# Block-diagonal products cut into 64-row halves side by side, in a two-layer attention kernel with a hand-written order

## The chip, the cores and the metric

The kernel runs on one core of one Trainium2 chip. The metric is the time of the whole program on the device in microseconds, as the median of several runs. A profiled execution of the same program gives the times of the single instructions.

## The reference

The input `x` has 2048 tokens of width 512, in bfloat16, with 32 heads of 16. Two layers, A and B, are applied twice each: `x += A(layernorm(x))`, `x += B(layernorm(x))`, and both again with the same weights.

Layer A cuts the tokens into four segments of 512. Inside a segment it is causal softmax attention; across segments it keeps a memory `M` (16 x 16 per head) and a vector `z`:

```python
for s in range(4):
    p = softmax(qs @ ks.T * scale + mask);  a_dot = p @ vs
    pq = phi(qs)                       # phi(t) = t+1 if t > 0 else exp(t)
    a_mem = (pq @ M) / (pq @ z + 1e-6)
    o = g * a_mem + (1 - g) * a_dot    # g = sigmoid(beta), one per head
    pk = phi(ks);  M += pk.T @ vs;  z += pk.sum(0)
```

The outputs go through `wo`. In the first segment the memory is zero, so it is computed only for segments 1 to 3.

Layer B is linear attention without a mask. Queries and keys pass through a 16 x 16 matrix per head, and their features are `[softmax(p), softmax(-p)]`, 32 per head. `kv` (32 x 16 per head) and `z` are sums over all 2048 keys; `num = phi_q @ kv`, `den = phi_q @ z + 1e-6`, and `num / den` goes through `wo`.

## The kernel before

The program is a list of operations (`Graph.op`) that the Python code makes in a natural order. Each names the tiles it reads and writes. `Graph.place` then decodes a table, `ORDER`: the position of each operation in one global order, the engine of each (some copies out of PSUM may go to ScalarE or VectorE), and the buffer that each tile gets. `Graph.emit` writes one program per engine in that order, with semaphore waits where an operand comes from elsewhere. So the order on each engine is fixed by the table; nothing is chosen on the chip.

128 tokens are one step. Heads lie in groups of eight (`NG` = 4 groups, 8 x 16 = 128 partitions). Segments are indexed `s`, the steps in a segment `i`, the rounds `L` (0 and 1). In layer B the chunks of 512 tokens are `c`.

PSUM has two pools. `pD` holds two tiles of 1024 float32 (two banks each): attention scores, layer B's query projections and layer B's numerators. `pG` holds four single banks: projections, score-value products (`pv`, two of the four at a time), and a class `nz`.

Layer A's attention, `a_att`, works per step and head group. Scores of a key block (`Sd` for the diagonal, `S` for the others) are products of 64 rows: two halves of the array, each with four heads, write different banks of a D tile. ScalarE takes the exponential, and score-value products, also of 64 rows, add up in the two `pv` banks. The line of all these products is that of the helper `mm` (L325), so the profile tells them apart by tiles: `D<-pK,pQ` scores, `D<-tri,two` the causal mask, `G<-pV` and `G<-pW` score-value products.

The memory part of `a_att` (segments 1 to 3, 24 steps over both rounds) has, per step, a group `NMd` of denominator products into columns 288 to 320 of the first `pv` bank (one product of `eps32` and `onesb` for the 1e-6, and four of 8 columns, 128 rows high), a reciprocal of 32 values on VectorE (L369), a group `NM` of four products of 128 rows by 128 columns into an `nz` bank, the product with the reciprocals (L794) into a tile `nmt`, and the sum with the attention result (L796). `MSb` is the memory in block-diagonal form: each group of 128 rows holds eight heads, and a head's rows are zero outside its own 17 columns.

Layer B's `b_query` works per chunk. The queries are projected (`D<-pX,WB_q`), exponentials with both signs go into `EQ`, and `Zq` products with `Rz1` give the sums for the denominators; a short chain of ScalarE and VectorE operations on 128 columns makes two weights per head and token, `AB`. Then for each of the four steps `N` is eight products of 128 rows by 128 columns (four groups, two signs) of `EQ` with the block-diagonal `Rkv`, into a D tile (`D<-Rkv,p`). ScalarE copies it to SBUF (`Nev`), VectorE weights it (`nmul`, L961) and adds the two signs (`nadd`, L967). For the steps in `PE_T` the addition is made by TensorE, while transposing (`pair`, L808). `out_proj` transposes and multiplies with `WB["o"]`, whose rows were loaded in the order that the head layout needs.

The projections, the output products and the transposes by TensorE are 128 rows high.

The DMA queue of the SP engine carries loads, transposes (`L344`), half swaps (`pW<-pV`) and stores.

## Time and profile before

| | |
|---|---|
| median of the runs | 500.85 us (499.58, 500.85, 501.59) |
| profiled execution, first to last instruction | 497.1 us |
| around that span, by the median | 3.75 us |
| TensorE clock granted | 1.000 |
| busy: TensorE / VectorE / ScalarE / GpSimd | 469.4 / 438.1 / 440.9 / 58.8 us |
| numerators of layer B, `D<-Rkv,p` 128x128 | 256 products |
| memory products, `G<-MSb,p` 128x128 and 128x8 | 96 and 96 products |
| score and other exponentials of 1024 columns | 256, mean 1045 ns |
| loads of `WB["o"]` on SP | 4, 128 KB each |

The profile names engines PE (TensorE products), PEld (their weight loads), DVE (VectorE), ACT (ScalarE), POOL (GpSimd) and SP. A product's busy time contains the latency of the array; starts that follow each other closely tell what one costs. "64*128 64x128" is a product of 64 rows, 128 stationary columns and 128 moving columns. `p` stands for several SBUF pools, whose digits are left out.

### The profile page before, as it was taken

Reading aid. Unit: us, or ns where it says so; the run is one execution under the profiler, and the core shown is the slowest. Engines: PE = TensorE matmul, PEld = TensorE weight load, DVE = VectorE, ACT = ScalarE, POOL = GpSimd, SP = SyncE. Lnnn points to the kernel's source line nnn. Section 1 sums busy time; section 2 is a strip of 40 time slices with the busy share of each in tenths; the row PEclk is TensorE's granted clock in tenths of the full one; section 3 lists DMA queues with packets and bytes.
Section 4 is the critical chain, followed back from the end, with each engine's and each line's share of the span. In section 5 each row is a group of like instructions: output and inputs, shape, how many; then the busy total and the mean of one; then the engine's idle time right before and its main releaser. Section 6 shows DMA issues by size and latency. Waiting matters only on the chain.

```text
span 497.1 us, 22749 instructions
## 1 busy us (share of the span) xinstructions
PE 469.4 (94%) x10186; PEld 299.8 (60%) x10282; DVE 438.1 (88%) x1115; ACT 440.9 (89%) x611; POOL 58.8 (12%) x142
## 2 busy tenths in 40 slices
PE   9989999999999989999999999999999999999896
PEld 4446665566676676557555665467566757656652
DVE  7989999998778969987999999999797899889885
ACT  3889999997999989489999999999999998966992
POOL 4512201000001101001220221010001011010000
PEclk9999999999999999999999999999999999999999
DMA  8986733211112031000243444321303112110155
GB/s 227 251 142 89 81 76 47 61 27 38 41 31 53 7 47 36 12 1 1 45 75 74 82 79 69 63 47 34 58 11 50 37 34 34 26 24 2 44 113 164
DMA packets 89377, 30.20 MB, mean 61 GB/s; under 512 B 75936, under 2 KB 89280, under 8 KB 89280
## 3 DMA queue, kind: packets, MB, share of 16 engines
q1 hardware_dynamic: 88928, 28.46, 30.2%
q8 instruction: 80, 1.31, 1.1%
q10 hardware_dynamic: 288, 0.26, 0.2%
q14 instruction: 17, 0.14, 0.1%
q0 software_dynamic: 64, 0.02, 0.1%
HBM read 6.32 MB, written 2.10 MB: 17 GB/s over the span
## 4 chain that ended last, share of the span: by engine, by line
PE 61%; ACT 24%; DVE 9%; issue 3%; DMA 2%; SPq 0%; POOL 0%
PE G L325 41%; PE D L325 18%; ACT p L331 16%; ACT pE L331 6%; DMA X<-in_A_x_dram 1%; DVE p L961 1%; DVE X L826 1%; DVE pS L887 1%; DMA pX<-p 1%; DVE stats L552 1%; PE G L808 1%; DVE WA_v L508 1%; DVE pQ L642 1%; DVE pT L869 0%; ACT WB_v L339 0%
## 5 line engine op out<-in xcount | busy, mean ns | idle before, releaser
L331 ACT ACTIVATE p<-D 128x1024 bf16<-128x1024 f32 x256 | 255.6, 1045 | 13.6 <-PE D L325 12.4
L325 PE MATMUL D<-pK,pQ 64*128 64x128 bf16 (+1 forms) x2560 | 112.3, 212 | 2.9 <-ACT pE L331 0.7
L331 ACT ACTIVATE pE<-D 128x768 bf16<-128x768 f32 x128 | 104.0, 840 | 9.8 <-PE D L325 9.0
L325 PEld LDWEIGHTS D<-pK,pQ 64*128 64x128 bf16 x2560 | 70.9, 94 | 54.9 <-ACT p L331 20.5
L325 PE MATMUL G<-pV,p 64*128 64x34 bf16 (+1 forms) x1632 | 78.9, 178 | 0.5 <-ACT pE L331 0.2
L331 ACT ACTIVATE p<-G 128x512 bf16<-128x512 f32 x112 | 69.0, 633 | 7.8 <-PE G L325 7.0
L325 PEld LDWEIGHTS G<-pV,p 64*128 64x128 bf16 (+1 forms) x1632 | 70.4, 93 | 7.3 <-issue 2.6
L325 PE MATMUL G<-pV,pE 64*128 64x34 bf16 x1024 | 73.0, 175 | 1.5 <-issue 1.5
L325 PE MATMUL G<-pW,pE 64*128 64x34 bf16 x1024 | 71.3, 175 | 0.6 <-issue 0.5
L325 PE MATMUL G<-pW,p 64*128 64x34 bf16 x1536 | 70.4, 176 | 0.8 <-issue 0.8
L325 PEld LDWEIGHTS G<-pW,p 64*128 64x128 bf16 x1536 | 63.8, 93 | 0.8 <-issue 0.4
L560 POOL TENSOR_SCALAR rstd<-mv 128x1 f32<-128x1 f32 x60 | 15.5, 261 | 379.6 <-DVE mv L553 379.6
L325 PEld LDWEIGHTS G<-pV,pE 64*128 64x128 bf16 x1024 | 53.3, 93 | 3.3 <-issue 3.2
L325 PEld LDWEIGHTS G<-pW,pE 64*128 64x128 bf16 x1024 | 50.5, 92 | 0.7 <-issue 0.7
L552 DVE BATCH_NORM_STATS2 stats<-X 128x6 f32<-128x512 bf16 x64 | 43.3, 682 | 3.1 <-DMA X<-in_A_x_dram 2.5
L642 DVE TENSOR_SCALAR pQ<-p,m 128x512 bf16<-128x512 bf16 x128 | 40.8, 340 | 2.6 <-PE D L325 1.6
L887 DVE TENSOR_REDUCE pS<-p 128x32 f32<-128x512 bf16 x64 | 41.7, 671 | 0.9 <-ACT p L331 0.6
L826 DVE TENSOR_TENSOR X<-X,G 128x512 bf16<-128x512 bf16 x48 | 32.5, 682 | 10.6 <-PE G L325 10.2
L869 DVE TENSOR_TENSOR pT<-G,pT 128x1024 bf16<-128x1024 f32 x30 | 36.2, 1212 | 2.3 <-PE G L325 1.9
L562 POOL TENSOR_TENSOR rstd<-rstd,mhalf 128x1 f32<-128x1 f32 x60 | 36.0, 605 | 3.7
L325 PE MATMUL D<-tri,two 64*128 64x256 bf16 x256 | 35.1, 270 | 0.0
L325 PE MATMUL G<-WA_v,pX 128*128 128x512 bf16 x128 | 32.9, 381 | 0.6 <-DVE WA_v L508 0.5
(118 smaller groups left out, 839.6 us busy)
## 6 DMA issues: line engine op xcount, KB each, us to landing
pW<-pV SPq DMA_DIRECT2D x16, 136.0 KB, 3.2
out_dram<-X SPq DMA_DIRECT2D x16, 128.0 KB, 1.8
X<-in_A_x_dram SPq DMA_DIRECT2D x3, 512.0 KB, 7.4
pX<-in_B_wqkv_dram SPq DMA_DIRECT2D x3, 512.0 KB, 7.3
p<-p SPq DMA_TRANSPOSE x76, 2.5
pX<-p SPq DMA_TRANSPOSE x54, 2.5
WA_k<-in_A_wk_dram SPq DMA_DIRECT2D x2, 256.0 KB, 7.5
WA_v<-in_A_wv_dram SPq DMA_DIRECT2D x1, 512.0 KB, 8.4
```

What stands on the lines that cost most here:

```text
L325: ins = e.matmul(out_ap, lhsT, rhs, start=st, stop=sp, tile_position=(basep(lhsT), basep(out_ap)))
L331: return self.g.op({"act": (dur, lambda e: e.activation(out_ap(), in_ap(), func, scale=scale))}, reads, writes, opens, label=label)
L508: fn = lambda e, dt=dt: e.tensor_tensor(self.WA["v"][:, dt, :].rearrange("p (h d) -> p h d", h=H), self.WA["v"][:, dt, :].rearrange("p (h ...
L552: v(lambda e: e.bn_stats(self.stats[:, t, :], self.X[:, t, :]), 602, [R("X", t)], [R("st", t)], label="bn")
L560: v(lambda e: e.tensor_scalar(rs, self.mv[:, t, 1:2], LN_EPS, None, op0=ALU.add), 170, [R("mv", t)], [R("rstd", t)], eng="pool", label="rstd")
L562: v(lambda e: e.tensor_tensor(rs, rs, self.mhalf[:], ALU.pow), 540, [R("rstd", t), R("mhalf")], [R("rstd", t)], eng="pool", label="rstd")
L642: fn = lambda e, KM=KM, KT=KT, sl=sl: e.tensor_scalar(KM.t[:, :, sl % 2, :, 64 * (sl // 2):64 * (sl // 2) + 64], KT.t[:].rearrange("p (j h ...
L808: ins = e.matmul(tp.t[:, k * 128:(k + 1) * 128], pair.t[:, sgn * 512 + k * 128:sgn * 512 + (k + 1) * 128], self.ident[:], start=sgn == 0, ...
L826: self.v(lambda e: e.tensor_tensor(self.X[:, t, :], self.X[:, t, :], ps.t[:, 0:512], ALU.add), 602, [R("X", t), ps[0]], [R("X", t)], label ...
L869: v(lambda e: e.tensor_tensor(dst(), ps.t[:, None, 0:512].to_broadcast([128, 2, 512]).rearrange("p s (g d h) -> p s g d h", g=NG, h=8), rz ...
L887: fn = lambda e, sgn=sgn, E=E, Z=Z: e.tensor_reduce(Z.t[:, sgn * 32:(sgn + 1) * 32], E.t[:, sgn * 512:(sgn + 1) * 512].rearrange("p (h d) ...
L961: v(lambda e, Ns=Ns, Tm=Tm, w=w, shape=shape: e.tensor_tensor(shape(Tm.t[:]), shape(Ns.t[:]), w(), ALU.mult), 600, [Ns, AB[0], AB[1]], [Tm ...
```

## The change

Layer B: each numerator block becomes sixteen products of 64 rows by 64 columns, the upper and the lower half of the rows in turn, each half into its own bank of the D tile. A half holds four of a group's eight heads, so it reads only their columns of `Rkv`. Results lie by half, sign and group; the weights `AB`, the sum of the signs, the paired transposition and the rows of `WB["o"]` (loaded in eight pieces) follow that layout.

Layer A: a new function `a_mem` runs for every second step. For a segment it makes all denominators at once, 16 products of 8 columns in an `nz` bank, and takes their reciprocals on ScalarE as the exponential of a negative logarithm, kept in `Rm` (in pool `pS`). For each two steps it makes 16 products of 64 rows by 64 columns into a D tile and multiplies the 1024 results with the reciprocals on VectorE in one instruction, into a tile of pool `p2`. `a_att` only adds.

The order table is new. Decoded, it has 3017 operations where the old one has 3067: TensorE 984 (1014), ScalarE 614 (612), VectorE 1088 (1115), GpSimd 139 (138), SP 192 (188).

```diff
-        self.eps32 = sb("eps32", [128, H], BF16)
+        self.eps6 = sb("eps6", [128, 1], F32)
...
         for g in range(NG):
-            load(lambda g=g: [(self.WB["o"][:, g, :], inp["B_wo"][g * 128:(g + 1) * 128, :].rearrange("(h d) o -> d h o", d=16))],
-                 128, [R("WBo", g)])
+            for hf in range(2):
+                load(lambda g=g, hf=hf: [(self.WB["o"][64 * (g % 2):64 * (g % 2) + 64, 2 * hf + g // 2, :],
+                                          inp["B_wo"][g * 128 + hf * 64:g * 128 + hf * 64 + 64, :].rearrange("(h d) o -> d h o", d=16))],
+                     64, [R("WBo", g, hf)])
...
+    def a_mem(self, L, s, i):
...
+        if i == 0:
+            st["mem"] = []
+            Rm = st["rm"] = self.T(self.pS, "Rm")
+            mc = self.T(self.pG, "nz")
+            col = lambda q, g: mc.t[:, (q // 2) * 64:(q // 2) * 64 + 64].rearrange("p (a t g h) -> p a t g h", a=2, t=2, g=NG)[:, :, q % 2, g, :]
+            self.mm(lambda: [(col(q, g), PQ[g].t[:, q * 128:(q + 1) * 128], self.MSb[mb][:, g, :, 16], True, True)
+                             for q in range(4) for g in range(NG)], [8] * 16, list(PQ) + ms, [mc], opens=[Rm], label="NMd")
+            self.g.op({"act": (158.0, lambda e: e.activation(Rm.t[:, 0:128], mc.t[:, 0:128], ACT.Ln, bias=self.eps6[:, 0:1]))},
+                      [mc, R("eps6")], [Rm], label="mln")
+            self.act(lambda: Rm.t[:, 128:256], lambda: Rm.t[:, 0:128], ACT.Exp, 128, [Rm], [Rm], scale=-1.0, psum=False, label="mln")
+        Rm = st["rm"]
+        NM = self.T(self.pD, "S")
+        tmp = self.T(self.p2, "nmt")
+        st["mem"].append(tmp)
+        self.mm(lambda: [(NM.t[:, hf * 512 + (q - i) * 256 + g * 64:hf * 512 + (q - i) * 256 + g * 64 + 64], PQ[g].t[64 * hf:64 * hf + 64, q * 128:(q + 1) * 128],
+                          self.MSb[mb][64 * hf:64 * hf + 64, g, 4 * hf:4 * hf + 4, 0:16], True, True) for q in (i, i + 1) for g in range(NG) for hf in range(2)],
+                [], list(PQ) + ms, [NM], opens=[tmp], label="NM", rows=64, dur=240)
+        v(lambda e: e.tensor_tensor(tmp.t[:].rearrange("p (h d) -> p h d", d=16), NM.t[:, :].rearrange("p (h d) -> p h d", d=16),
+                                    Rm.t[:, 128 + 32 * i:192 + 32 * i][:, :, None].to_broadcast([128, 64, DH]), ALU.mult), 1131, [NM, Rm], [tmp], label="nmn")
...
+        if s >= 1 and i % 2 == 0:
+            self.a_mem(L, s, i)
         PV = [self.T(self.pG, "pv") for _ in range(2)]
...
-        if s >= 1:
-            PQ = st["PhQ"]
-            mc = lambda: PV[0].t[:, 288:320]
-            self.mm(lambda: [(mc(), self.onesb[:], self.eps32[:], True, False)] +
-                    [(PV[0].t[:, 288 + 8 * g:296 + 8 * g], PQ[g].t[:, i * 128:(i + 1) * 128], self.MSb[mb][:, g, :, 16], False, g == NG - 1) for g in range(NG)],
-                    [32] + [8] * 4, list(PQ) + [R("MSb", mb, 0), R("MSb", mb, 1), R("onesb"), R("eps8")], [PV[0]["d"]], label="NMd")
...
         if s >= 1:
-            v(lambda e: self.recip(e, rmem(), mc()), self.dur_recip(32), [PV[0]["d"]], [Rt[2]], label="rden")
-            NM = self.T(self.pG, "nz")
-            tmp = self.T(self.p1, "nmt")
-            self.mm(lambda: [(NM.t[:, g * 128:(g + 1) * 128], st["PhQ"][g].t[:, i * 128:(i + 1) * 128], self.MSb[mb][:, g, :, 0:16], True, True)
-                             for g in range(NG)], [128] * 4, list(st["PhQ"]) + [R("MSb", mb, 0), R("MSb", mb, 1)], [NM], opens=[tmp], label="NM")
-            v(lambda e: e.tensor_tensor(tmp.t[:].rearrange("p (h d) -> p h d", h=H), NM.t[:, :].rearrange("p (h d) -> p h d", h=H),
-                                        rmem()[:, :, None].to_broadcast([128, H, DH]), ALU.mult), 602, [NM, Rt[2]], [tmp], label="nmn")
-            v(lambda e: e.tensor_tensor(o.t[:], o.t[:], tmp.t[:], ALU.add), 335, [o[0], o[1], tmp], [o[0], o[1]], label="oadd", port=True)
+            tmp = st["mem"][i // 2]
+            hv = lambda x: x.rearrange("p (g a c) -> p a g c", g=NG, a=2)
+            mv = lambda: tmp.t[:].rearrange("p (a t g c) -> p a t g c", a=2, t=2, g=NG)[:, :, i % 2]
+            v(lambda e: e.tensor_tensor(hv(o.t[:]), hv(o.t[:]), mv(), ALU.add), 335, [o[0], o[1], tmp], [o[0], o[1]], label="oadd", port=True)
...
-            self.mm(lambda tt=tt, N=N: [(N.t[:, sgn * 512 + g * 128:sgn * 512 + (g + 1) * 128],
-                                         EQ[(g // 2, sgn)].t[:, (g % 2) * 512 + tt * 128:(g % 2) * 512 + (tt + 1) * 128],
-                                         self.Rkv[:, g * 2 + sgn, :, :], True, True) for sgn in range(2) for g in range(NG)],
-                    [128] * 8, list(EQ.values()) + [R("Rkv", q) for q in range(3)], [N], opens=[Tm] + ([] if pair else [o]), label="N")
-            shape = lambda x: x.rearrange("p (k d h) -> p k d h", k=2 * NG, h=8)
+            self.mm(lambda tt=tt, N=N: [(N.t[:, hf * 512 + sgn * 256 + g * 64:hf * 512 + sgn * 256 + (g + 1) * 64],
+                                         EQ[(g // 2, sgn)].t[64 * hf:64 * hf + 64, (g % 2) * 512 + tt * 128:(g % 2) * 512 + (tt + 1) * 128],
+                                         self.Rkv[64 * hf:64 * hf + 64, g * 2 + sgn, :, 4 * hf:4 * hf + 4], True, True)
+                                        for sgn in range(2) for g in range(NG) for hf in range(2)],
+                    [], list(EQ.values()) + [R("Rkv", q) for q in range(3)], [N], opens=[Tm] + ([] if pair else [o]), label="N", rows=64, dur=240)
+            shape = lambda x: x.rearrange("p (k d h) -> p k d h", k=4 * NG, h=4)
...
             if not pair:
-              v(lambda e, Tm=Tm, o=o: e.tensor_tensor(o.t[:], Tm.t[:, 0:512], Tm.t[:, 512:1024], ALU.add), 335, [Tm], [o], label="nadd", port=True)
+              v(lambda e, Tm=Tm, o=o: e.tensor_tensor(o.t[:].rearrange("p (a c) -> p a c", a=2), half(Tm, 0), half(Tm, 1), ALU.add), 335, [Tm], [o], label="nadd", port=True)
...
 ORDER = """
...
```

## The prediction, made before the result was known

> **What bounds the kernel now.** I read the page's busy times and its chain first, then the busy times by stage, the chain inside each stage, the matmul starts around the two product blocks that change, the groups of VectorE, and ScalarE's waits.

> The page, sections 1 and 4:

> ```profile
> PE 469.4 (94%) x10186; PEld 299.8 (60%) x10282; DVE 438.1 (88%) x1115; ACT 440.9 (89%) x611; POOL 58.8 (12%) x142
> PE 61%; ACT 24%; DVE 9%; issue 3%; DMA 2%; SPq 0%; POOL 0%
> ```

> Three engines are nearly full, and the chain runs through TensorE for 61% of the span. Busy times in five stretches (time; PE, PEld, DVE, ACT, POOL busy): layer A with memory in the first round, layer B's queries in the first round, layer A with memory in the second, the end.

> ```profile
> 75.00:205.00 130.00, 123.64 (x3261) 83.09 (x3286) 113.50 (x274) 118.99 (x157) 9.56 (x24) 1.00 0.21 38
> 205.00:275.00 70.00, 68.55 (x738) 40.41 (x748) 63.38 (x172) 62.81 (x97) 10.33 (x23) 1.00 0.18 36
> ...
> 312.00:440.00 128.00, 122.50 (x3323) 82.09 (x3349) 112.80 (x276) 118.10 (x153) 10.17 (x26) 1.00 0.22 38
> 440.00:497.00 57.00, 50.97 (x498) 30.55 (x502) 46.09 (x102) 41.75 (x62) 0.79 (x2) 1.00 0.31 75
> ```

> The chain of waits in the first two of these, by line:

> ```profile
> by line: PE G L325 57.6%; PE D L325 22.1%; ACT p L331 11.3%; ACT pE L331 4.9%; issue 4.1%; ACT pK L339 0.4%
> by line: PE G L325 53.7%; PE D L325 31.5%; ACT p L331 5.8%; PE G L808 2.7%; PE G L358 1.6%; issue 1.5%; DVE p L784 1.0%; DVE X L340 0.9%; ACT pS L331 0.7%; DVE pS L369 0.3%; DVE p L601 0.3%; DVE mv L553 0.2%
> ```

> So TensorE carries 80% of the chain in the first memory stage and 89% in the first query stage; the same view of 312 to 440 us gives it 64% (44.6 + 19.2). These shares are my weights: a microsecond taken from TensorE there is worth 0.80, 0.89 and 0.64 us. In the end stage layer B's numerators run between 460 and 485 us, and there ScalarE's timeline goes from one instruction into the next (463.5 to 476.8 us without a gap of note), so TensorE time is worth little.

> Busy TensorE time contains pipeline latency, so I price matmuls by the distance of their starts. The TensorE timeline (start, length) around a memory product, and around a numerator block of layer B:

> ```profile
> 121.31 0.33 PE L325 MATMUL D<-pK,pQ 64*128 64x128 bf16 x8
> 121.48 0.27 PE L325 MATMUL D<-tri,two 64*128 64x256 bf16 x2
> 121.69 0.41 PE L325 MATMUL G<-MSb,p 128*128 128x128 bf16 x4
> 121.93 0.18 PE L325 MATMUL G<-eps,onesb 128*128 128x32 bf16 x1
> 121.96 0.26 PE L325 MATMUL G<-MSb,p 128*128 128x8 bf16 x4
> 122.07 0.59 PE L325 MATMUL G<-WA_v,pX 128*128 128x512 bf16 x2
> ```

> ```profile
> 225.77 0.62 PE L808 MATMUL G<-ident,p 128*128 128x128 bf16 x8
> 226.23 0.61 PE L325 MATMUL D<-Rkv,p 128*128 128x128 bf16 x8
> 226.68 0.61 PE L808 MATMUL G<-ident,p 128*128 128x128 bf16 x8
> ```

> Four prices follow. (a) A 128-row numerator product takes 0.45 / 8 = 0.056 us. (b) The eight 64-row score products at 121.31 (two pairs of 128 columns, two of 64) take 0.17 us: pairs do run side by side, and a pair of 64 columns costs (0.17 - 2 x 0.056) / 2 = 0.029 us. (c) The two 256-column mask products run side by side too and need 256 / 128 x 0.056 = 0.11 us, yet the next start is 0.21 us later: going from 64-row to 128-row work costs 0.10 us. Over the 159 changes in each direction the median excess between starts is 0.096 us into 64 rows and 0.094 us out. From numerators to other 128-row work (226.23 to 226.68) it costs nothing. (d) A memory product costs 0.24 / 4 = 0.059 us, a denominator product 0.026 us.

> **Layer B numerators.** A block of eight (0.45 us) becomes eight pairs (0.23 us): 0.22 us less. But its neighbours are 128-row projections and transposes, so an isolated block now pays two changes of height, 0.19 us, and gains 0.03. Two blocks in a row (there are two D tiles to hold them) gain 0.25 together. For 32 blocks that is 1.0 to 4.0 us; the trace before has 26 runs for the 32 blocks, and with that clustering it is 7.0 - 26 x 0.19 = 2.1 us. I take 2.1, half in each round: 1.05 x 0.89 = 0.9 in the first, 0.2 in the second, where ScalarE is the limit.

> [...] Without the changes of height the first round's term would be 3.5 x 0.89 = 3.1 us and not 0.9.

> The moving operand is now read in runs of four columns, which no row shows. Bounds: 0.029 us a pair, or no overlap, 0.056; then a block saves nothing and costs 0.19 us, 6.1 us in all. I take 0.029, since runs of 16 (price d) cost only 0.003 more than contiguous columns.

> **Layer A memory products.** 96 products at 0.059 become 96 pairs at 0.029: 2.9 us less. 24 denominator groups of 0.029 + 4 x 0.026 = 0.133 us become 96 products of 0.026: 0.7 less. Striking these blocks from the sequence of starts removes 24 of the 318 changes of height (2.3 us); the six new denominator groups put back at most 12 (1.1 us), and the products now have the height of the score products beside them. Together 4.8 us, half in each round: 2.4 x 0.80 = 1.9 and 2.4 x 0.64 = 1.5.

> **VectorE and ScalarE.**

> ```profile
> L869 DVE TENSOR_TENSOR pT<-G,pT 128x1024 bf16<-128x1024 f32 x30 | 36.2, 1212 | 2.3 <-PE G L325 1.9
> L961 DVE TENSOR_TENSOR p<-p,pS 128x1024 bf16<-128x1024 bf16 x32 | 21.8, 685 | 0.5 <-ACT p L331 0.2
> L794 DVE TENSOR_TENSOR p<-G,pS 128x512 bf16<-128x512 f32 x24 | 16.4, 685 | 3.3 <-PE G L325 2.8 <-issue 0.2
> L369 DVE RECIPROCAL pS<-G 128x32 f32<-128x32 f32 x24 | 8.2, 342 | 0.2
> ```

> Gone: 24 reciprocals (8.2 us) and 24 products from PSUM (16.4). New: 12 double products, priced by the 1024-element PSUM row, 14.5. The new table's operations per engine, against those that the code adds and drops (VectorE -36, ScalarE +12), say that ten more copies go from ScalarE to VectorE (+6.9 and -6.2 us) and one weight product from VectorE to GpSimd (-1.5). The logarithm and exponential per segment cost ScalarE 6 x (0.30 + 0.32) = 3.7. VectorE -4.7, ScalarE -2.5; with chain shares of about 6% and 17% in the memory stages, 0.7 us.

> The numerators' weighting at L961 keeps its 685 ns only if runs of four weights are as good as eight. No row has four; the far bound is the 1212 ns row, 32 x 0.53 = 17 us of VectorE. I take 685, since the row it is nearest to differs only in run length. [...]

> **The price of the D tiles.** Memory products move from a G bank to one of the two D tiles through which scores reach ScalarE:

> ```profile
> ACT p L331 <- PE D L325: 12.4, 26, 3.8
> ACT pE L331 <- PE D L325: 9.0, 18, 1.4
> ```

> ScalarE waits 21.4 us in all for D today. A memory tile holds its D for 0.23 (products) + 0.2 (latency, from the 219 ns product rows) + 1.21 (the multiply), 1.6 us. Meanwhile the scores use one tile: after an exponential of 1.05 us the next needs a score block, 0.2 + 0.2 us, before it can start. That is nothing if a copy or a key exponential from G (0.6 us) lies there, 0.4 if not, 0.8 if the multiply also queues for another microsecond on VectorE. 12 tiles: 0 to 9.6 us. I take 0.1 each, 1.2, twice today's mean wait of 21.4 / 384 = 0.06 a tile.

> **At nothing.** Strided adds at L796 and L967 keep runs of 64 and 256 elements. The denominators no longer sit in a score-value bank, which frees it 0.34 us earlier, 24 times. Layer B's output weights load in eight pieces for four: four more issues of 0.6 us on SP's queue, first needed at 227 us; if they stand ahead of a transpose in the first 30 us, up to 2.4 us. The weight product on GpSimd: up to 1 us at the start.

> **The sum**: 0.9 + 0.2 + 1.9 + 1.5 + 0.7 - 1.2 = 4.0 us. The profiled execution's 497.1 us span becomes 493.1; the median of the runs, 3.75 us above that span (launch and end), goes from 500.85 to 496.9.

> **Rivals.** *Slower, by the D tiles*: each memory tile costs 0.8 us of ScalarE and its scores; 500.85 - 5.2 + 9.6 = 505.3. It decides from 0.43 us a tile (the gain is gone) and shows as slower from 0.64. For it: 21.4 us of waits on D already, and VectorE 88% full. Against: over the kernel ScalarE has 112 exponentials and some 60 copies from G to put in between. Chance 0.20. *Hidden*: ScalarE is 92% busy in both memory stages, so freed TensorE time becomes waiting and only ScalarE's 2.5 us less, partly, remains: 499.6. Chance 0.16. *The numerators lose*: no overlap; first round 3.05 x 0.89, second 0.5: 500.85 + 3.2 - 4.1 + 1.2 = 501.2. Chance 0.08. *All three engines shed alike*, with paired numerators: TensorE 8.8 of 469 us, 1.9% of the span, 491.5. Chance 0.12. The forecast has 0.44, with its own range 493.5 to 499.5.

> This kernel's measurement tells about 0.5%, 2.5 us, from no change. Faster by more: the forecast less a tail of 0.05, the last rival, 0.02 of the hidden case, 0.53. Within: 0.23. Slower: the D tiles and 0.04 of the others, 0.24. The range of 490 to 505.5 leaves out half of the D case and the ends of the others.

> **What the changed profile would show.** Right: numerator products of 64x64 about 0.03 us a pair with 0.1 us gaps around each run; ScalarE's waits for D near 22 us; the L961 form at 685 ns. Wrong: waits for D of 27 us or more, pairs of 0.056 us, or a weighting of 1.2 us.

## The result, and the profile after

The changed kernel takes 538.95 us (median of 4 runs, 532.95 to 541.87) against 500.22 us (4 runs) before. The ratio, taken without the slowest run of 541.87 us, which is also the profiled one, is 1.0717, 95% interval 1.0643 to 1.0792. It is 7% slower; 496.9 us was forecast, and the range ended at 505.5. The profiled execution of the changed kernel took 541.87 us with a span of 540.1 us, at a mean granted TensorE clock of 0.971 (before: 497.1 us, 1.000).

The page after, sections 1, 3 and 4:

```profile
PE 471.1 (87%) x10515; PEld 294.6 (55%) x10610; DVE 438.3 (81%) x1088; ACT 442.3 (82%) x613; POOL 62.9 (12%) x143
...
q8 instruction: 83, 1.36, 1.1%
...
PE 53%; DVE 20%; DMA 13%; issue 4%; ACT 4%; SPq 3%; POOL 2%; POOLq 0%; DVEq 0%
```

Busy time is what it was (TensorE 469.4, VectorE 438.1, ScalarE 440.9 us before). The 43 us are added idle time on each of the three engines. The chain shows where: DMA had 2% of it and now has 13%, GpSimd and SP's queue come in, and ScalarE falls from 24% to 4%.

The waits after (engine, line, waited for: us in total, times, longest):

```profile
ACT p L331 <- PE D L325: 29.2, 35, 4.1
...
ACT pE L331 <- PE D L325: 23.0, 31, 3.5
...
PE G L325 <- DMA pX<-p: 15.3, 10, 3.8
...
PE G L325 <- DMA p<-p: 13.5, 9, 2.8
```

ScalarE's waits for D rise from 21.4 to 52.2 us, far over the 27 us that the prediction named as the sign of its D rival. But TensorE itself now waits for transposes: with a third group (one wait of 3.8 us for `pX<-pX`) and 1.2 us of small ones 33.8 us. Before it was this one wait:

```profile
PE G L325 <- DMA pX<-p: 0.9, 1, 0.9
```

In the timeline of TensorE's two rows and SP's queue this looks so:

```profile
428.40 2.10 SPq L344 DMA_TRANSPOSE p<-p  x1
...
430.54 1.62 SPq L344 DMA_TRANSPOSE pX<-p  x1
...
434.11 1.19 SPq L344 DMA_TRANSPOSE p<-p  x1
...
435.16 0.13 PEld L325 LDWEIGHTS G<-WB_k,pX 128*128 128x128 bf16 x2 [3.96 <-DMA pX<-p]
435.16 1.46 PE L325 MATMUL G<-WB_k,pX 128*128 128x512 bf16 x3 [3.84 <-DMA pX<-p]
```

A key projection of layer B stands next in TensorE's queue. Its input was ready for transposing at 420.9 us; SP issued the transpose only at 430.5, behind others, and TensorE stood from 431.3 to 435.2.

One more row changed: the clock that TensorE was granted. In the profile before it is 1.00 throughout. After, it is 0.50 in seven stretches, 31 us in all, and six of them overlap a gap of 1.6 to 4.1 us between the starts of two weight loads or follow it within 1 us. Two stretches, the one around the end of the wait above and the next (the clock is the third number from the end):

```profile
433.66:440.49 6.83, 5.33 (x38) 2.13 (x38) 1.19 (x4) 2.49 (x4) 0.00 (x0) 0.50 0.11 20
440.49:447.00 6.51, 6.19 (x153) 3.80 (x154) 4.53 (x6) 6.19 (x9) 0.00 (x0) 1.00 0.01 3
```

In the stretches at 0.50, products of 128 rows and 512 columns start 0.43 us apart (median of 19), elsewhere 0.22 (of 781). What this is worth can only be estimated. Call a run's time multiplied by one minus its granted clock its clock loss. Over 133 runs of the kernels of this document, each compared with the others of its kernel and chip, a run with 1 us more of clock loss is 0.8 us longer. The changed kernel's four runs lose 13.1 us on average, the kernel before 0.9 to 2.2 us in its five sets of runs. By this estimate some 9 of the 38.7 us came with the clock. No run here held the clock fixed, and that the waits bring it down is not shown: at four other such gaps of the same profile, of 1.9 to 3.2 us (they end at 83.2, 277.9, 344.6 and 462.5 us), the clock is 1.00.

The prices of the new operations by form:

```profile
L985 DVE TENSOR_TENSOR p<-p,pS 128x1024 bf16<-128x1024 bf16 x32 | 21.5, 682 | 0.6 <-ACT p L331 0.5
...
L729 DVE TENSOR_TENSOR p<-D,pS 128x1024 bf16<-128x1024 f32 x12 | 14.7, 1222 | 4.6 <-PE D L325 4.1 <-ACT pS L331 0.5
...
L325 PE MATMUL D<-Rkv,p 64*128 64x64 bf16 x512 | 13.0, 201 | 0.5 <-DVE Rkv L864 0.4
```

### The profile page after: what moved, and what is told of

Same layout as the page of the kernel before. It is cut to its first block, busy times and chain, and to the rows that moved or that the text cites. A ratio compares the mean times of both kernels' runs of the same rounds, so it can differ in the third digit from the quotient of the medians.

```text
span 540.1 us, 23380 instructions
## 1 busy us (share of the span) xinstructions
PE 471.1 (87%) x10515; PEld 294.6 (55%) x10610; DVE 438.3 (81%) x1088; ACT 442.3 (82%) x613; POOL 62.9 (12%) x143
## 4 chain that ended last, share of the span: by engine, by line
PE 53%; DVE 20%; DMA 13%; issue 4%; ACT 4%; SPq 3%; POOL 2%; POOLq 0%; DVEq 0%
PE G L325 36%; PE D L325 16%; DMA pX<-p 7%; DMA p<-p 4%; ACT p L331 3%; DVE stats L554 2%; SPq L344 2%; DVE X L845 2%; DVE p L985 2%; DVE pQ L644 1%; DVE pS L906 1%; DVE pT L888 1%; DMA beta_sb<-in_A_beta_dram 1%; DMA pX<-pX 1%; DVE p L340 1%
## 5 line engine op out<-in xcount | busy, mean ns | idle before, releaser
L331 ACT ACTIVATE p<-D 128x1024 bf16<-128x1024 f32 x256 | 254.1, 1035 | 30.1 <-PE D L325 29.2
L331 ACT ACTIVATE pE<-D 128x768 bf16<-128x768 f32 x128 | 102.2, 821 | 23.4 <-PE D L325 23.0
L325 PE MATMUL D<-pK,pQ 64*128 64x128 bf16 (+1 forms) x2560 | 114.5, 214 | 2.6 <-DVE pQ L644 1.1
L325 PEld LDWEIGHTS D<-pK,pQ 64*128 64x128 bf16 x2560 | 72.5, 95 | 57.1 <-issue 23.3
L325 PE MATMUL G<-pV,p 64*128 64x34 bf16 (+1 forms) x1632 | 79.9, 179 | 3.3 <-issue 2.9
L331 ACT ACTIVATE p<-G 128x512 bf16<-128x512 f32 x112 | 67.2, 615 | 16.9 <-PE G L325 15.2
L325 PEld LDWEIGHTS G<-pV,p 64*128 64x128 bf16 (+1 forms) x1632 | 71.8, 93 | 8.8 <-issue 5.3
L325 PE MATMUL G<-pV,pE 64*128 64x34 bf16 x1024 | 73.9, 176 | 2.5 <-DMA pW<-pV 1.2
L325 PE MATMUL G<-pW,p 64*128 64x34 bf16 x1536 | 71.2, 176 | 3.0 <-issue 2.9
L325 PE MATMUL G<-pW,pE 64*128 64x34 bf16 x1024 | 72.1, 176 | 0.0
L325 PEld LDWEIGHTS G<-pW,p 64*128 64x128 bf16 x1536 | 65.1, 93 | 3.3 <-issue 2.9
L562 POOL TENSOR_SCALAR rstd<-mv 128x1 f32<-128x1 f32 x60 | 18.8, 316 | 412.8 <-DVE mv L555 405.6
L325 PEld LDWEIGHTS G<-pV,pE 64*128 64x128 bf16 x1024 | 53.9, 93 | 4.3 <-issue 2.8
L325 PEld LDWEIGHTS G<-pW,pE 64*128 64x128 bf16 x1024 | 51.1, 93 | 0.2
L325 PE MATMUL G<-WB_k,pX 128*128 128x512 bf16 x111 | 30.9, 397 | 13.4 <-DMA pX<-p 11.5
L888 DVE TENSOR_TENSOR pT<-G,pT 128x1024 bf16<-128x1024 f32 x30 | 36.2, 1215 | 5.8 <-PE G L325 5.8
L325 PE MATMUL G<-WA_o,p 128*128 128x512 bf16 x112 | 30.5, 390 | 10.6 <-DMA p<-p 7.6
L325 PE MATMUL G<-WB_o,p 128*128 128x512 bf16 x120 | 32.4, 395 | 7.0 <-DMA p<-p 5.0
```

The lines of the kernel that those rows point to most:

```text
L325: ins = e.matmul(out_ap, lhsT, rhs, start=st, stop=sp, tile_position=(basep(lhsT), basep(out_ap)))
L331: return self.g.op({"act": (dur, lambda e: e.activation(out_ap(), in_ap(), func, scale=scale))}, reads, writes, opens, label=label)
L562: v(lambda e: e.tensor_scalar(rs, self.mv[:, t, 1:2], LN_EPS, None, op0=ALU.add), 170, [R("mv", t)], [R("rstd", t)], eng="pool", label="rstd")
L888: v(lambda e: e.tensor_tensor(dst(), ps.t[:, None, 0:512].to_broadcast([128, 2, 512]).rearrange("p s (g d h) -> p s g d h", g=NG, h=8), rz ...
```

## The experiments

Two numbers are followed through all runs, besides the time. *Transposes*: the time that TensorE waits for a DMA transpose or swap (0.9 us before, 33.8 after). *Pauses*: gaps of 0.7 us and more between the starts of two weight loads, from 8 us on, where the second carries no wait on a semaphore (none before; 12 after, 12.9 us in all). The kernels of the experiments ran on four chips, each beside runs of the kernel before, whose medians there are 499.55 to 501.96 us. So kernels of different groups are better compared by their ratios than by their medians.

| kernel | us, median | ratio to before, 95% | transposes, us | pauses: number, us |
|---|---|---|---|---|
| changed | 538.95 | 1.0717 [1.0643, 1.0792] | 33.8 | 12, 12.9 |
| numerators_old_order | 503.62 | 1.0050 [1.0019, 1.0082] | 3.6 | 1, 0.7 |
| memory_old_order | 520.74 | 1.0364 [1.0266, 1.0462] | 2.6 | 5, 7.1 |
| both_old_order | 521.19 | 1.0394 [1.0328, 1.0461] | 7.4 | 6, 6.4 |
| memory_new_order | 541.65 | 1.0791 [1.0723, 1.0859] | 29.8 | 9, 10.8 |
| memory_in_G | 507.46 | 1.0143 [1.0087, 1.0199] | 0.9 | 2, 2.3 |
| wide_memory_in_D | 513.75 | 1.0271 [1.0216, 1.0325] | 1.0 | 0 |
| changed_resequenced | 523.21 | 1.0469 [1.0403, 1.0535] | 2.9 | 11, 12.8 |
| before_resequenced | 516.19 | 1.0320 [1.0262, 1.0378] | 0.6 | 2, 2.5 |
| before_shifted | 517.59 | 1.0327 [1.0258, 1.0397] | 9.1 | 9, 11.6 |
| memory_old_order_shifted | 518.70 | 1.0350 [1.0307, 1.0393] | 3.1 | 6, 6.1 |
| changed_shifted | 537.56 | 1.0723 [1.0655, 1.0791] | 27.6 | 7, 10.6 |
| changed_no_memory_products | 539.17 | 1.0756 [1.0699, 1.0813] | 32.6 | 7, 8.1 |
| before_shifted_a_packet | 500.69 | 1.0007 [0.9967, 1.0047] | 0.4 | 1, 0.7 |
| memory_in_G_aligned | 508.86 | 1.0148 [1.0087, 1.0209] | 1.3 | 1, 0.7 |
| wide_memory_in_D_aligned | 514.97 | 1.0286 [1.0218, 1.0354] | 1.9 | 0 |
| both_in_G_aligned | 509.05 | 1.0164 [1.0099, 1.0230] | 0.9 | 2, 1.7 |
| before_shifted_quarter | 508.61 | 1.0148 [1.0085, 1.0211] | 7.6 | 1, 1.3 |
| changed_shifted_quarter | 532.21 | 1.0641 [1.0573, 1.0708] | 24.9 | 9, 11.7 |

### The parts in the old order, and one part in the new

Theory: the new order table costs the time. Rival: the D tiles do, as in the prediction's slower case. Four kernels: each part alone in the old order (its new operations at the places of those that they replace), both there, and the memory part in the new order with 128-row numerators.

```diff
 both_old_order:        a_mem and N as in the change;  ORDER: old
 numerators_old_order:  N as in the change, memory as before;  ORDER: old
 memory_old_order:      a_mem as in the change, N as before;  ORDER: old
 memory_new_order:      a_mem as in the change, N as before;  ORDER: new
```

> All edits of the change, but in the old order: every operation that both kernels have keeps its place, engine and buffer of the old table; the 6 denominator groups, 12 double memory products and their multiplies are put in near the old memory products, where a D tile is free. Theory 'order' (the edits cost about nothing, the new table's sequence costs the 39 us): 496 to 508 us, TensorE waits for DMA transposes below 5 us as before. Theory 'edits' (D tiles and changes of height cost it): 520 us or more, with ScalarE waiting over 40 us for D.

> Layer B's numerators alone as 64-row pairs, with the new weight layout, all in the old order (operations one for one; the eight weight loads stand where the four stood); layer A as before. Theory 'order': 498 to 502 us, the forecast's term of about one microsecond less. Theory 'edits' by changes of height: 505 or more, about 0.2 us or more for each of 32 blocks.

> Layer A's memory part alone as in the change, in the old order with the same insertions; layer B as before. Theory 'order' with the forecast's price of a D tile: 496 to 501 us. Theory 'D tiles': each of the 12 costs 0.8 us or more, 505 us or more, and ScalarE's waits for D grow from 21 us to over 30.

> Layer B's numerators back as 128-row products, everything else as changed, in the new table's order one for one. Theory 'order': still 530 to 545 us. Theory 'numerators' (their changes of height in the new order cost it): 525 us or less.

Neither theory holds alone. The memory part costs 18 to 20 us in the old order; the new order adds 16 to 18 to the whole (1.0394 to 1.0717, 521.19 to 538.95 us). With both parts in the old order the time lies in the range of the theory "edits", but ScalarE's waits for D are 35.4 us, not over 40. The numerators alone, at 503.62 us, lie between the two ranges, some 2.5 us above before, and in the new order the kernels with and without them do not differ clearly (1.0717 and 1.0791, with intervals that overlap): they are not the cause.

How a memory product meets the D tile in memory_old_order (timeline of TensorE, VectorE, ScalarE):

```profile
345.31 0.42 PE L325 MATMUL D<-MSb,p 64*128 64x64 bf16 x16 [0.30 <-ACT pE L331]
...
345.77 1.23 DVE L727 TENSOR_TENSOR p<-D,pS 128x1024 bf16<-128x1024 f32 x1 [0.66 <-PE D L325]
...
347.05 0.45 PE L325 MATMUL D<-pK,pQ 64*128 64x128 bf16 x10 [0.36 <-DVE p L727]
...
347.49 1.02 ACT L331 ACTIVATE p<-D 128x1024 bf16<-128x1024 f32 x1 [0.16 <-PE D L325]
```

The tile is taken from 345.31 to 347.00 and the next score product starts 0.05 us later. Over the 12 tiles the hold, from the first weight load to the end of the multiply, is 1.85 us on average (the prediction's 1.6), and eleven of the 12 next score products start within 0.25 us of the release. In the changed kernel itself the next score products come 0.04 to 3.9 us after the release, and TensorE works on other products up to the start of each of the 12.

### The memory part taken apart

Theory: the D tile costs its hold. Rivals: the products of 64 rows, or the early denominators with their reciprocals on ScalarE.

```diff
 memory_in_G (old order; NMd and mln as in the change)
-        NM = self.T(self.pD, "S")          # two steps, 64 rows side by side
+        NM = self.T(self.pG, "nz")         # per step, 4 products of 128 rows
 wide_memory_in_D (table of memory_old_order)
-            NM.t[:, hf * 512 + ...], PQ[g].t[64 * hf:64 * hf + 64, ...]   # 16 of 64 x 64
+            NM.t[:, (q - i) * 512 + g * 128:...], PQ[g].t[:, ...]         # 8 of 128 x 128
```

> Layer A's memory part with the denominators of a segment in one go and their reciprocals on ACT, as in the change, but the products step by step in a bank of G at 128 rows, at the places in the order that they had before; layer B as before. D-tile theory (a memory product that takes one of the two D tiles holds up the exponentials by about 1.5 us, 12 times): no D tile is taken, so 497 to 503 us, ratio 0.99 to 1.005, and ACT's waits for PE at D return to about 21 us in all. Rival (the denominators early, the ACT reciprocals or the strided weights cost it): 512 us or more, as in memory_old_order.

> As memory_old_order, instruction for instruction in the same order and the same buffers, but the memory products of two steps are 8 products of 128 rows by 128 columns instead of 16 of 64 by 64 side by side. D-tile theory: 518 to 526 us (520.7 with 64 rows; each tile is held some 0.2 us longer and two changes of height go away). Rival (the 64-row products and their changes of height are what costs 20 us): 500 to 507 us.

Both fall between the theories, and three steps come out. **Denominators and reciprocals, 1.4%**, some 7 us, are there with no D tile taken. **The D tiles**: the two kernels have the same products, 513.75 - 507.46 = 6.3 us, 0.5 us for each of 12. **64 rows for 128**: 520.74 against 513.75 us, by the ratios 1.0364 against 1.0271, so 5 to 7 us, though the narrow version's products are shorter (0.23 us to the last start against 0.42) and its tile is held less. The two ran on different chips and their intervals overlap, so this step is the least certain of the three. The first is seen on ScalarE in memory_in_G:

```profile
165.71 1.93 ACT L331 ACTIVATE p<-D 128x1024 bf16<-128x1024 f32 x2
167.99 0.37 ACT L717 ACTIVATE pS<-G,eps 128x128 f32<-128x128 f32 x1 [0.35 <-PE G L325]
168.39 0.31 ACT L331 ACTIVATE pS<-pS 128x128 f32<-128x128 f32 x1
168.61 0.58 ACT L331 ACTIVATE p<-G 128x512 bf16<-128x512 f32 x1
```

The logarithm waits for the denominators and takes 0.37 us, the exponential 0.31, and everything behind them on ScalarE moves by that: over six segments 4.1 us of work and 1.4 of waits. The rest of the 7 us has no row of its own.

The third had no row at first: TensorE's pauses in memory_old_order are named "issue", a wait for nothing that the profile shows. There are five, 7.1 us, and none in the wide version. The clock differs too: the narrow version loses 4.0 us to it on average and the wide one 1.2, by the estimate above some 2 us of the step.

### The sequence alone

```diff
 changed_resequenced:  operations, engines and buffers of the changed kernel;  ORDER: positions sorted anew
 before_resequenced:   the same for the kernel before
```

> The changed kernel with the same instructions on the same engines in the same buffers; only the sequence of the instructions is sorted anew, by a search over single moves that replays the durations measured in the two traces. Sequence theory (the new table places products before their transposes have landed, and the memory products between two exponentials that need the D tile): the time falls below 515 us, ACT's waits for D fall from 52 us to under 30, PE's waits for transposes from 33 us to under 12. D-tile theory with a fixed price of 1.5 us a tile whatever the sequence: 518 to 525 us. If neither holds (the buffers and engines of the new table are to blame): 530 us or more.

> The kernel before, sorted anew by the same search with the same effort: what the sequence alone is worth without any edit. Sequence theory: it gains less than the changed kernel does, as its sequence was timed for its code: 485 to 500 us. If the search merely fits its own replay: 500 us or more.

The changed kernel gains 15.7 us, with no edit but the sequence. That is less than the sequence theory asked for: 523.21 us lies in the range of the D-tile theory, 518 to 525, and not below 515. Its chain and its waits:

```profile
PE 57%; DVE 23%; ACT 9%; issue 4%; DMA 3%; SPq 2%; POOL 1%; DVEq 0%
```

```profile
ACT p L331 <- PE D L325: 20.6, 41, 1.8
...
ACT pE L331 <- PE D L325: 12.4, 19, 1.5
```

The waits for transposes are gone (33.8 to 2.9 us), as the sequence theory says. ScalarE's for D fall to 33.0, not under 30; the pauses stay (12.8 us); the clock loss falls from 13.1 to 7.2 us. But the kernel before lost 16 us by the same treatment. Its second expectation holds: that search fitted its own replay of durations. With two pauses, 2.5 us, and 0.6 us of waits for transposes, no run shows what the old sequence does better. So 15.7 us is what a sequence without late transposes gives the changed kernel, not a best value. With both kernels sorted by the same search, the changed one is 7 us slower (523.21 against 516.19, on one chip).

### What the pauses are

The instruction queue moves 83 packets of 16,384 bytes in the changed kernel, and TensorE has 10,610 weight loads, as many products and 126 semaphore instructions there: 63.7 bytes for each. From that the author's estimate is 64 bytes for an instruction and 256 instructions in a packet. Theory: TensorE pauses where the next packet has not landed. The program begins with warm-up products that nothing reads; cut into more and shorter ones, they shift all later instructions against the packets. What the cut itself costs is seen in the shift by 256, at a ratio of 1.0007.

```diff
         for k in range(N_WARM):
-            unit(128, 512, 1)
+            if k < 9:                      # a packet: k < 16, unit(128, 56, 9);  a quarter: k < 4, the same
+                unit(128, 64, 8)
+            else:
+                unit(128, 512, 1)
```

> The kernel before, in which nine of the warm-up products of 512 columns at the start are each written as eight of 64 columns: the same TensorE time within 0.2 us, but every later TensorE instruction stands 126 instructions further on. Fetch theory (TensorE pauses without any wait where the next 16 KB of its instructions have not landed): pauses of 0.7 us and more, of which before has none, appear or not as the boundaries fall, and the time changes by their sum: 497 to 504 us. Rival (the pauses have another cause): no pause, same time within 0.5%.

> memory_old_order with the same shift by 126 TensorE instructions. Fetch theory: its five pauses without a wait (7.1 us in all, next to the products that follow 188.9, 292.3, 353.2, 389.7 and 453.0 us) move to other products or go; the time differs from 520.7 us by about what their sum changes, so 512 to 526 us, and each pause again ends 1.2 to 1.5 us after a 16 KB packet of the instruction queue has landed. Rival: the same five pauses at the same products, 519 to 523 us.

> The changed kernel with the same shift. Fetch theory: its twelve pauses of 0.7 us and more (12.9 us in all) change places, their number stays near ten since the products stand as thickly as before, 532 to 545 us. Rival: the same pauses before the same products, 539 us within 0.5%.

> The kernel before with the warm-up products cut so that every later TensorE instruction stands 256 further on: 256 instructions of 64 bytes are one packet of 16384 bytes, so the boundaries fall on the same products again. Alignment theory: no pause of 0.7 us or more, 498 to 503 us, against 517.6 with half a packet (126). Rival (any shift, or the cut warm-up itself, costs 16 us): 512 us or more.

The kernel before takes 3.3% longer with a shift of 126 instructions and the same time with 256. The pauses appear, as the theory says, but the time is far above its 497 to 504 us: beside 11.6 us of pauses, the waits for transposes rose by 8.2. One of the nine pauses, in the timeline of weight loads:

```profile
184.15 0.20 PEld L325 LDWEIGHTS D<-pK,pQ 64*128 64x128 bf16 x8
...
184.46 0.09 PEld L325 LDWEIGHTS G<-pW,p 64*128 64x128 bf16 x1
186.23 0.09 PEld L325 LDWEIGHTS G<-pV,p 64*128 64x128 bf16 x1 [1.68 <-issue]
...
186.47 0.21 PEld L325 LDWEIGHTS D<-pK,pQ 64*128 64x128 bf16 x8
```

The same score products in the kernel before, with the same group of weighted values between them:

```profile
179.32 0.22 PEld L325 LDWEIGHTS D<-pK,pQ 64*128 64x128 bf16 x8
...
180.02 0.20 PEld L325 LDWEIGHTS D<-pK,pQ 64*128 64x128 bf16 x8
```

0.70 us became 2.32, in the middle of a group that waits for nothing. The DMA view of the shifted kernel from 183.3 to 184.9 us has one instruction packet, from 183.36 to 184.82:

```profile
q8 instruction: 1, 0.02, 5.7%
```

TensorE starts again 1.41 us after that landing. The 17 kernels that have such pauses have 91, and 87 of them end 0.8 to 1.7 us after a landing. Of these, 86 stand at instruction 193 or 194 modulo 256 (counted by the weight loads, since a few traces lack records of products), all twelve of the changed kernel among them: the period of the estimate, which is why these places are called boundaries here. In before_shifted, changed, changed_resequenced and memory_old_order the time from the start of that fetch to TensorE's restart is 2.2 to 3.0 us, and only some 25 to 270 instructions were left when it started. Where products follow each other in pairs every 0.03 us (four instructions) 150 of them last 1.1 us, and the rest is the pause.

So the 64-row memory products go with five pauses at such places, 7.1 us in memory_old_order, and the 128-row products of wide_memory_in_D with none. That this is their whole cost is not shown: no run had the narrow memory products without pauses. The shifted memory_old_order has six pauses in place of five, at other products. The changed kernel has 7 to 12 at every shift tried, and 11 when resequenced, with hardly a late transpose, so the late transposes are not what makes the pauses.

### What is left once the boundaries fall as before

```diff
-  for q in range(4) for g in range(NG)], [8] * 16, ...          # NMd
+  for q in (0, 1, 2, 3, 0) for g in range(NG)], [8] * 20, ...   # four products twice: as many instructions as before
```

> memory_in_G with four of the 16 denominator products of each segment computed twice (into the same columns, with the same values), so that a segment has as many TensorE instructions as before and the packets' boundaries fall as before again, but for up to 30 instructions inside a segment. Alignment theory: 499 to 503 us, at most one pause of 0.7 us. Rival (the early denominators and ACT's reciprocals cost the 7 us of memory_in_G): 506 to 509 us.

> wide_memory_in_D with the same four products repeated: the products of memory_in_G_aligned, but in tiles of D. The difference of the two is the price of the D tiles alone with aligned fetches. If it is 0.5 us a tile, as 513.75 less 507.46 says: 505 to 509 us; if the tile costs its hold of 1.5 us and more: 517 us or more; if alignment was all: 499 to 503 us.

> The best of the parts, to beat before: layer B's numerators as 64-row products (16 more TensorE instructions a block, 256 a pass, so aligned again after each pass) with memory_in_G_aligned, in the old order. Alignment theory and the prediction's terms of the numerators (-1.1) and denominators (-0.7): 497 to 503 us. Rival: the costs of the parts add up, 507 us or more.

The alignment theory misses for memory_in_G: one pause of 0.7 us is left and the time stays at 1.0148, so the 7 us belong to its denominators and reciprocals. The D tiles come out at 514.97 - 508.86 = 6.1 us, 0.5 us each, a second time; the time itself misses the 505 to 509 us of that expectation, which counted on the alignment. With the numerators added in the best form the whole is 509.05 us: no version of the change that was run beats the kernel before.

### The tiles in the new order, and a third shift

```diff
 changed_no_memory_products
-        self.mm(... [NM], ..., label="NM")     # 16 products in a tile of D
-        v(... tmp = NM.t * Rm ...)
+        v(... tmp = Rm * Rm ...)               # same size and place
```

> The changed kernel without layer A's memory products: the 12 groups of 16 products are left out and the weighting on DVE multiplies the reciprocals with themselves, so that it keeps its place and its size but no tile of D is taken (the memory's share of the output is not computed). Sequence theory (the new table covers the hold of the D tile; its cost lies in products that stand before their transposes have landed): 530 to 538 us. D-tile theory, at 1.6 us a tile in this order too: 516 to 522 us.

> The kernel before with every later TensorE instruction 64 further on, a quarter of a packet. Alignment theory: with 0 and 256 there was no pause of 0.7 us or more but for one of 0.74 us, with 126 nine; a quarter lies between: 503 to 518 us, and the time above 500.9 us is about the sum of the pauses, up to half as much again. Rival (only a shift by half a packet hurts): 499 to 503 us.

> The changed kernel with the same quarter of a packet. Alignment theory: 530 to 545 us, as with 0 (538.95) and 126 (537.56), since its products stand as thickly wherever the boundaries fall. If the changed kernel had an alignment as good as that of before, it would show as a run with few pauses below 528 us.

Without the memory products the changed kernel takes the same time, just above the range of the sequence theory and far from the D-tile theory's 516 to 522 us. ScalarE still waits for D:

```profile
ACT p L331 <- PE D L325: 33.7, 38, 4.2
...
ACT pE L331 <- PE D L325: 16.5, 27, 3.5
```

With no memory product in a tile, these 50.2 us are waits for scores that TensorE computes late. So in the new order a price of 1.6 us a tile is excluded. A price of a few microseconds in all is not: leaving out 384 instructions also moved the boundaries (7 pauses for 12), and the clock loss is 18.5 us in place of 13.1, by the estimate above some 4 us, which can hide a gain of that size.

A quarter of a packet costs the kernel before 1.5%, with only one long pause of 1.3 us, so the time is not the sum of the pauses, as was expected; 7.6 us of waits for transposes came with it, and why is not settled. The changed kernel has 538.95, 537.56 and 532.21 us at the three shifts, the kernel before 500.22, 517.59 and 508.61: before is in a good alignment, and the change is slower by 20 to 39 us at each.

## Why the prediction was wrong

**The new order was taken as neutral.** This is the step that failed first. Every term was worked out for a place in the old sequence, and the moves on SP's queue stood under "at nothing" with bounds of a few microseconds. In the new sequence products stand in TensorE's queue before their transposes have landed (33.8 us of waits); with the edits the same, the new order takes 16 to 18 us more than the old one, and sorting alone takes 15.7 us away. The decoded table was used to count operations per engine; it could have been asked how far each product stands behind its transpose.

**The pauses had no term.** The sum priced products by the distance of their starts, and there the prices were right: pairs every 0.030 to 0.031 us (0.029 in the sum), 0.096 us for a change of height into 64 rows (median of 169) and 0.093 out (median of the 96 whose next product has its record in the trace). But 328 more products (10,610 weight loads for 10,282) mean 656 more instructions, and moved boundaries. In the kernel before a shift alone costs 16 us, with pauses of 11.6 us; in the changed kernel the pauses are 12.9 us long, and what they are worth there is open.

**The clock had no term either.** The sum was taken off a span with a granted clock of 1.00 throughout. The changed kernel had 0.971 to 0.983, by the estimate above some 9 us.

**VectorE and ScalarE, a gain of 0.7 us**, had the wrong sign: the part that puts reciprocals on ScalarE costs 7 us in the old order. The two operations were priced about right (0.62 us, measured 0.68) but set against copies that leave ScalarE, and weighted by its chain share of 17%; they stand in ScalarE's queue between exponentials, where 5.5 of the 7 us are seen as their length and the first one's wait for the denominators.

**The price of the D tiles** had the right mechanism and hold, and bounds of 0 to 0.8 us that hold the measured 0.5. The value taken, 0.1, came from the mean wait of a tile in a kernel that has no other holder. In the old order 12 x 0.5 is the rival's 0.43 "from which the gain is gone"; in the new order it is below 1.6 us a tile and not settled further. The rival's sign in the profile, waits for D over 27 us, came true for another cause.

**Right**: the price of the height of the products, the weighting at L985 (682 ns for runs of four, 685 for runs of eight before), and no overlap lost in the numerators.

What is accounted for: in the old order 7 (reciprocals) + 6 (D tiles) + 5 to 7 (the 64-row form, with its pauses and its clock) make up the memory part's 18 to 20 us. In the new order 15.7 of 38.7 us is the sequence. The other 23 us hold the pauses, the reciprocals, some of the clock loss and perhaps the D tiles. These runs do not divide them further, since no run of the changed kernel was without pauses and none had the memory products of the new order in G.

## What to carry to other kernels

When a change brings a new hand-made or searched order, price the order itself: for each product, how far its transposes are issued ahead on their queue, and run the old code and the new order apart before reading any other term. A kernel whose order was chosen by time on the chip may sit in a good place relative to its instruction packets, as the kernel before did here (1.0327 with a shift of 126 instructions, 1.0007 with 256); shift it by some 126 harmless instructions, to see how much of a difference is the edit. Read the granted clock of each run beside its time before giving a few microseconds to an edit. Price work moved to a buffer or an engine that the critical alternation uses at its place in that queue: here mean shares and mean waits gave a gain of 0.7 us for the reciprocals on ScalarE and 0.1 us for a D tile, and the old order paid 7 us and 0.5 us a tile.
